# Gates worked out per expert tile from logits in the scattered row, the rank-one term of feature 128 on VectorE, and low parts of the expert weights on GpSimd

## The chip, the cores and the metric

The kernel runs on one core of a Trainium2 chip. The metric is the device time of one execution in microseconds (us). Five engines work side by side, each through its own queue in order: TensorE (PE) multiplies matrices, with its weight loads shown apart as PEld; VectorE (DVE), ScalarE (ACT) and GpSimd (POOL) work on elements; SyncE (SP) issues most of the transfers between the main memory and the on-chip buffer. An engine waits at an instruction until what it needs has been signalled, and what stands behind it in its queue waits too.

## The reference

Three steps follow one another on 8 x 3072 = 24576 tokens of 256 features: the real part of a two-dimensional Fourier transform of each batch, a product layer, and a layer of 8 experts with one expert per token.

```
X = fft(fft(x, axis=1), axis=2).real            # 8 x 3072 x 256
h = ((X @ w1) * (X @ w2)) @ w3 @ w_out          # w1, w2: 256 x 1024, w3: 1024 x 1024, w_out: 1024 x 256
xn = h / (norm(h) + 1e-6);  en = emb / (norm(emb) + 1e-6)
logits = xn @ en.T / tau                        # 8 experts
e = argmax(logits);  gate = softmax(logits)[e]  # sum + 1e-9
out = gate * (relu(h @ ew1[e]) @ ew2[e])        # ew1: 256 x 1024, ew2: 1024 x 256
```

The gate of the chosen expert is 1 / (sum of exp(logit - largest logit) + 1e-9), so it needs the logits and the norm of the token's row.

## The kernel before

Numbers in fp32 are split in a high part, rounded by ScalarE, and a low part, the rest, subtracted by another engine (`split`, lines 112 and 115); a product is then three matmuls (high by high, low by high, high by low). A name that ends in `h` or `l` is such a part.

The program has four stages in the trace. Up to 305 us the Fourier transform runs over the sequence and, beside it, the weights are prepared: `w1` and `w2` are multiplied with the table of the second transform, `w3 @ w_out` is formed, and 8 columns are put behind it that give the logits before the norm. From 305 to 1562 runs the mid stage (`mid`), 24 chunks of 512 columns (tokens), each in 8 iterations. One iteration does three things. `stage_b` makes one slice `f` of 128 of the hidden features: matmuls into `p0`, `q0`, `p1`, `q1` (index 0 for `w1`, 1 for `w2`), sums and differences `a` and `b` of them, and their product `g` for two mirrored sets of columns. `just` splits 128 columns of the previous chunk's `g` into `jh` (ScalarE) and `jl` (POOL), and `stage_c` multiplies them with `wh` and `wl` in 24 matmuls 264 wide into `pc`, which ScalarE copies into `xs`. Two chunks later the router works on `xs`: `choose` finds each token's expert, `place` its slot in the expert's region, and `scatter` writes the token's row there, one indirect DMA of POOL for 128 tokens, 8 for a chunk.

The columns of the Fourier transform are symmetric, so 129 features carry all. Features 0 to 127 go through the matmuls. Feature 128 adds a rank-one term, a row of the columns times a column of the weights. For `w1` VectorE adds it when it empties `p0`: line 781, `ps0 = ub * wcol + p0`, where `ub` is the row in all partitions and `wcol` the weights. For `w2` PE adds it with one more matmul, `p1 <- ur, wrx`, of a three-row operand that is filled by small loads (lines 164 and 165), and ScalarE copies `p1` to `ps1` (line 785). After `stage_c`, ScalarE squares the row of each token with a running sum (line 817). `choose` takes from that the norm (`norm_of`, lines 129 to 139), divides the shifted logits by it (line 850), has ScalarE take the exponential (line 851), sums it and writes the gate behind the row, with the token's number behind that: 258 floats per row.

Beside the first chunks the 64 pieces of the expert weights, 128x512 each, are split by `presplit` (lines 892 to 897): a load `et`, its parts `eh` on ScalarE and `el` on VectorE, and two stores to `dex`. Each of the tiles has two buffers. The order of the engines is made by a scheduler when the program is built, not by the code's order. `mini` does the same work as the loop for one odd column.

After some work between the stages (1562 to 1690, with the first expert's tiles, `lead_tiles`), the expert stage runs over tiles of 256 tokens: `turn` transposes a tile by PE and splits it, `up` multiplies with `ew1` and applies relu while it splits (`hh` on ScalarE, `hl` on VectorE, line 1088), `down` calls `gated` for two halves, which multiplies with `ew2`, scales by the gate from the row (`o`, line 1102) and has POOL write the tokens' rows to the output.

Of the kernel before, what the change touches and what calls it, by code (L numbers as in the profile page):

```python
# [24 lines left out]
XW = 258  # L25
# [34 lines left out]
def fourier_experts(  # L60
# [80 lines left out]
    wcol = const.tile([128, FT], F32, name="wcol")  # L141
# [29 lines left out]
    def open_p1():  # L171
# [12 lines left out]
        wrx = p1c.tile([128, 4 * XW], F32R, name="wrx")  # L184
        nc.gpsimd.memset(wrx.bitcast(F32), 0.0)
        p1["wr"] = wrx[:, 0:F]
        p1["x"] = wrx.rearrange("p (a c) -> p a c", c=XW)
        nc.scalar.dma_start(out=wrx[0:3, 0:F].bitcast(F32), in_=dwr)
# [6 lines left out]
    with ExitStack() as c0:  # L195
        pz = c0.enter_context(tc.tile_pool(name="pz", bufs=2, reuse_waits="tile", space=PSUM))

        def side():
            with tc.tile_pool(name="pw1", bufs=1, reuse_waits="tile") as pe, \
# [7 lines left out]
                yield from prep_in(nc, tc, pr, pz, take, seven, split, prod, three, w1, w2, t_feat, t_row, dwr, wcol, dwc)  # L207
# [7 lines left out]
            nc, tc, c0, pz, split, prod, three, x, x128, xsp, (t_dft, t_pm), p1, du, dv, du128, du128f,  # L215
            dsp, dspx, side(),
        )
    with ExitStack() as c1:
        mid(
            nc, tc, c1, split, prod, three, norm_of, p1, wcol, du128, du128f, dw, dx, dex,  # L220
            ew1, ew2, t_tok, run, eg, lead, ident, out,
        )
# [60 lines left out]
def prep_in(nc, tc, pr, pz, take, seven, split, prod, three, w1, w2, t_feat, t_row, dwr, wcol, dwc):  # L283
    with tc.tile_pool(name="pa1", bufs=1, reuse_waits="tile") as pool, \
# [158 lines left out]
def dft(nc, tc, ctx, pz, split, prod, three, x, x128, xsp, tables, p1, du, dv, du128, du128f, dsp, dspx, side):  # L443
# [190 lines left out]
    def feature128():  # L634
# [24 lines left out]
        for g, c, w in GROUPS:  # L659
# [4 lines left out]
            r8 = [st.tile([NB, 386], F32R if i < 2 else F32, tag="o", name=f"r8{i}") for i in range(3)]  # L664
            split(r8[0][:, 0:n], r8[1][:, 0:n], ps[g][:NB, 0:n])
            nc.scalar.activation(out=r8[2][:, 0:n], in_=ps[g][:NB, 0:n], func=AF.Copy)
            for i, dst in ((2, du128f), (0, du128[:, 0]), (1, du128[:, 1])):
                nc.sync.dma_start(out=dst[:, c:c + w], in_=r8[i][:, 0:w].bitcast(F32))
                if g == 0:
                    nc.sync.dma_start(out=dst[:, H:H + 1], in_=r8[i][:, w:w + 1].bitcast(F32))  # L670
# [43 lines left out]
def mid(  # L714
    nc, tc, ctx, split, prod, three, norm_of, p1, wcol, du128, du128f, dw, dx, dex,
    ew1, ew2, t_tok, run, eg, lead, ident, out,
):
# [49 lines left out]
    def stage_b(f, ops, gt, c):  # L767
        uh, ul, vh, vl, ur, ub = ops
        fs = slice(f * 128, f * 128 + 128)
        ab = []  # L770
# [634 lines left out]
```

## Time and profile before

| | |
|---|---|
| median of 3 runs | 2751.56 us (2749.32 to 2752.73) |
| the profiled execution | 2768.9 us |
| its span, first to last instruction | 2767.2 us |
| mean granted TensorE clock | 0.976 |
| busy in the span: PE, PEld | 2602.1 (94%), 2441.5 (88%) |
| busy in the span: DVE, ACT, POOL | 1690.8 (61%), 1049.5 (38%), 1078.0 (39%) |

PE has work nearly all the time, but an average over four stages does not say which of them has room. Read it by stage: a stage in which PE is busy without a gap moves only with PE's own work; in a stage with gaps, the wait that ends last before PE's next matmul decides. Times in rows are counted from the span's start. "Idle before" with an arrow names what the engine was waiting for.

### The profile page before, as it was taken

What the parts mean: (1) busy time and instruction counts of PE and PEld (TensorE: products, weight loads), DVE (VectorE), ACT (ScalarE), POOL (GpSimd) and SP (SyncE); (2) the same over time, 40 slices, a digit from 0 to 9 for tenths busy, and PEclk for the clock granted to TensorE, in tenths of its full rate; (3) what the DMA queues carried; (4) which work ended last, traced back from release to release, by engine and by line L of the source; (5) the groups of instructions that cost most, each with busy time, mean ns of one, the idle gap of its engine ahead of it and who ended that gap; (6) DMA issues with size and microseconds to landing.
All of it is one profiled execution on the core that took longest, in us unless ns stands there. A gap on an engine that the chain in (4) does not pass through costs nothing.

```text
span 2767.2 us, 48866 instructions
## 1 busy us (share of the span) xinstructions
PE 2602.1 (94%) x18661; PEld 2441.5 (88%) x18661; DVE 1690.8 (61%) x3325; ACT 1049.5 (38%) x2069; POOL 1078.0 (39%) x748
## 2 busy tenths in 40 slices
PE   4988789999999999999999999999999999999998
PEld 3888677877888888888888899999999999999998
DVE  8999389999888878888888852222222222222222
ACT  3554234444434334434344433333333333333332
POOL 5465345565566555565565421111111111111111
PEclk7999899999999999999999999999999999999999
DMA  6766625455211011011010264111111422111110
GB/s 247 242 220 201 199 92 184 164 173 191 73 41 41 28 43 39 28 43 39 28 43 20 108 267 169 47 47 47 47 47 47 163 104 104 47 47 47 47 47 21
DMA packets 114249, 265.07 MB, mean 96 GB/s; under 512 B 16843, under 2 KB 55929, under 8 KB 109148
## 3 DMA queue, kind: packets, MB, share of 16 engines
q1 hardware_dynamic: 84670, 195.58, 21.5%
q0 software_dynamic: 19440, 51.35, 5.2%
q10 hardware_dynamic: 9902, 14.98, 1.5%
q8 instruction: 148, 2.42, 0.4%
q14 instruction: 89, 0.73, 0.1%
HBM read 521.17 MB, written 106.77 MB: 227 GB/s over the span
## 4 chain that ended last, share of the span: by engine, by line
issue 39%; PE 27%; DVE 17%; POOL 11%; DMA 3%; ACT 2%; POOLq 0%; SPq 0%; DVEq 0%; ACTq 0%
PE pc L122 14%; POOL out L1103 7%; PE p L122 6%; PE q L122 5%; DVE b L796 2%; DVE g L799 2%; POOL vl L115 2%; DMA et<-in 2%; DVE a L796 2%; PE acc L122 1%; DVE ps L781 1%; DVE el L115 1%; ACT jh L112 1%; DVE nrm L139 1%; POOL z L504 1%
## 5 line engine op out<-in xcount | busy, mean ns | idle before, releaser
L1088 DVE SCALAR_TENSOR_TENSOR hl<-pd,hh 128x512 fp32r<-128x512 f32 x396 | 273.8, 691 | 783.5 <-ACT hh L1087 752.6
L115 POOL TENSOR_TENSOR jl<-g,jh 128x1024 fp32r<-128x1024 f32 x184 | 443.0, 2409 | 393.9 <-ACT jh L112 330.2
L1103 POOL DMA_INDIRECT out<-o,x x192 | 187.3, 976 | 916.0 <-ACT o L1102 897.2
L122 PE MATMUL pc<-wh,jh 128*128 128x264 f32 x1536 | 449.9, 293 | 53.1 <-ACT xs L815 50.4
L122 PE MATMUL pc<-wh,jl 128*128 128x264 f32 x1536 | 444.1, 289 | 4.1 <-POOL jl L115 4.0
L122 PE MATMUL pc<-wl,jh 128*128 128x264 f32 x1536 | 442.7, 288 | 0.0
L1084 PE MATMUL pd<-xh,wt 128*128 128x256 f32 x2400 | 431.4, 278 | 0.0
L1100 PE MATMUL po<-wt,hh 128*128 128x256 f32 x2400 | 423.9, 280 | 0.0
L112 ACT ACTIVATE jh<-g 128x1024 fp32r<-128x1024 f32 x192 | 203.2, 1059 | 476.4 <-PE pc L122 350.7
L1084 PEld LDWEIGHTS pd<-xh,wt 128*128 128x128 f32 x2400 | 370.0, 188 | 0.0
L122 PEld LDWEIGHTS pc<-wh,jh 128*128 128x128 f32 x1536 | 296.4, 193 | 82.4 <-ACT xs L815 73.3
L1087 ACT ACTIVATE hh<-pd 128x512 fp32r<-128x512 f32 x396 | 236.7, 598 | 339.8 <-PE pd L1084 339.8
L1100 PEld LDWEIGHTS po<-wt,hh 128*128 128x128 f32 x2400 | 364.4, 188 | 0.0
L1100 PE MATMUL po<-wt,hl 128*128 128x256 f32 x1200 | 334.1, 278 | 0.0
L1084 PE MATMUL pd<-xl,wt 128*128 128x256 f32 x1200 | 333.9, 278 | 0.0
L122 PE MATMUL q<-vh,wc 128*128 128x512 f32 x768 | 308.0, 403 | 17.2 <-ACT a L794 10.6
L122 PE MATMUL p<-uh,wc 128*128 128x512 f32 x768 | 308.1, 402 | 3.7 <-DVE ps L781 3.6
L122 PEld LDWEIGHTS pc<-wl,jh 128*128 128x128 f32 x1536 | 296.9, 193 | 5.8
L122 PEld LDWEIGHTS pc<-wh,jl 128*128 128x128 f32 x1536 | 295.9, 193 | 5.6 <-POOL jl L115 5.4
L796 DVE TENSOR_TENSOR b<-ps,q 128x512 f32<-128x512 f32 x384 | 249.0, 688 | 33.9 <-ACT ps L785 20.3
L880 POOL DMA_INDIRECT dx<-xs,idx x192 | 192.5, 1003 | 154.3 <-DVE idx L876 82.0
L799 DVE TENSOR_TENSOR g<-a,b 128x512 f32<-128x512 f32 x384 | 247.6, 679 | 7.7 <-POOL a L796 7.5
(336 smaller groups left out, 5073.4 us busy)
## 6 DMA issues: line engine op xcount, KB each, us to landing
wt<-dex SPq DMA_DIRECT2D x75, 4096.0 KB
wc<-dex SPq DMA_DIRECT2D x22, 4096.0 KB
x<-dx SPq DMA_DIRECT2D x96, 258.0 KB
xt<-in SPq DMA_DIRECT2D x24, 1028.0 KB
et<-in SPq DMA_DIRECT2D x64, 256.0 KB
dex<-eh SPq DMA_DIRECT2D x64, 256.0 KB
dex<-el SPq DMA_DIRECT2D x64, 256.0 KB
raw<-in SPq DMA_DIRECT2D x28, 512.0 KB
```

What stands on the lines that cost most here:

```text
L112: nc.scalar.activation(out=hi, in_=src, func=AF.Copy)
L115: (lo_eng or nc.vector).tensor_tensor(out=lo, in0=src, in1=hi.bitcast(F32), op=ALU.subtract)
L122: nc.tensor.matmul(ps, lhsT=lh, rhs=rh, start=first and i == 0, stop=last and i == n - 1)
L139: nc.vector.scalar_tensor_tensor(out=n_, in0=n_, scalar=0.5, in1=t, op0=ALU.mult, op1=ALU.add)
L796: eng.tensor_tensor(out=t, in0=ps, in1=q, op=o)
L799: nc.vector.tensor_tensor(out=gt[sg][:, f, :], in0=ab[0][sg], in1=ab[1][sg], op=ALU.mult)
L880: i = nc.gpsimd.indirect_dma_start(out=dx, out_offset=bass.IndirectOffsetOnAxis(ap=idx[:, j if k is None else k:][:, 0:1], axis=0), in_=xs ...
L1084: nc.tensor.matmul(ps[:, a, :], lhsT=w[:, lh, o:o + 128], rhs=rh[:, k, :], start=i == 0, stop=i == 5)
L1087: nc.scalar.activation(out=hh[:, sl, :], in_=ps, func=AF.Relu)
L1088: nc.vector.scalar_tensor_tensor(out=hl[:, sl, :], in0=ps, scalar=0.0, in1=hh[:, sl, :].bitcast(F32), op0=ALU.max, op1=ALU.subtract)
L1100: nc.tensor.matmul(ps, lhsT=lh[:, f, sl], rhs=w[:, rh, c:c + D], start=i == 0, stop=i == 3 * FT - 1)
L1103: ins = nc.gpsimd.indirect_dma_start(out=out, out_offset=bass.IndirectOffsetOnAxis(ap=x[:, a, D + 1:D + 2].bitcast(U32), axis=0), in_=o, i ...
```

## The change

Three things change in the code.

- `stage_b` no longer has the matmul of the rank-one term for `w2`, and `ps1` is made as `ps0` was, by VectorE with `ub` and `wcol`, which now holds the column of both weight matrices. The three-row operands, their memory and their small loads go, in `mini` and in the preparation too.
- `choose` no longer works out the gate: the squares, the norm, the exponential and the reciprocals go from the mid stage. The row that `scatter` writes has the 256 features, the 8 logits and the token's number: 265 floats. The new function `gates` works the gates out for one tile of 256 tokens, in `turn` and in `lead_tiles`, and `gated` takes them. The tables of the expert stage share buffers.
- `presplit` has its low part `el` made by POOL.

The diff, cut to its core:

```diff
-XW = 258
+XW = 265
+XP = 272
+TK = 264
...
-    wcol = const.tile([128, FT], F32, name="wcol")
+    wcol = const.tile([128, 2, FT], F32, name="wcol")
...
-        ur = p1["ur"][p]
         ub = pool.tile([128, CH], F32, tag=f"ub{p}", name="ub")
-        nc.sync.dma_start(out=ur[0:1, :].bitcast(F32), in_=du128[b, 0:1, sl])
-        nc.sync.dma_start(out=ur[1:3, :].bitcast(F32), in_=du128[b, :, sl])
         nc.sync.dma_start(out=ub, in_=du128f[b:b + 1, sl].to_broadcast([128, CH]))
-        return ru, rv, ur, ub
+        return ru, rv, ub
...
+                nc.vector.tensor_copy(wcol[:, i, 4 * q:4 * q + 4], ps[:, 0:8:2])
...
-        uh, ul, vh, vl, ur, ub = ops
+        uh, ul, vh, vl, ub = ops
         fs = slice(f * 128, f * 128 + 128)
         ab = []
         for i in range(2):
             pp_ = pp.tile([128, CH], F32, tag=f"p{i}", name=f"p{i}")
-            terms = features(i, 0, f, (uh, ul), "u")
-            if i == 1:
-                terms.append((wr[:, fs], ur))
-            prod(pp_, terms)
+            prod(pp_, features(i, 0, f, (uh, ul), "u"))
             pq = pp.tile([128, CH], F32, tag=f"q{i}", name=f"q{i}")
             prod(pq, features(i, 1, f, (vh, vl), "v"))
             ps = wk.tile([128, CH], F32, tag=f"ps{i}", name=f"ps{i}")
-            if i == 0:
-                nc.vector.scalar_tensor_tensor(
-                    out=ps, in0=ub, scalar=wcol[:, f:f + 1], in1=pp_, op0=ALU.mult, op1=ALU.add
-                )
-            else:
-                nc.scalar.activation(out=ps, in_=pp_, func=AF.Copy)
+            nc.vector.scalar_tensor_tensor(
+                out=ps, in0=ub, scalar=wcol[:, i, f:f + 1], in1=pp_, op0=ALU.mult, op1=ALU.add
+            )
             pair, eng, q = [], nc.vector, pq
...
-        nc.scalar.activation(out=xs[:, j, :], in_=pc, func=AF.Copy)
-        jk = wk.tile([128, D], F32, tag="jk", name="jk")
-        nc.scalar.activation(out=jk, in_=xs[:, j, 0:D], func=AF.Square, accum_out=ss[:, j:j + 1])
+        nc.scalar.activation(out=xs[:, j, 0:TK], in_=pc, func=AF.Copy)
...
-        nrm = small("nrm", 1)[:, :nt]
-        norm_of(nrm, ss[:, :nt], ro, 128, nt, f"n{nt}")
-        nc.vector.tensor_scalar_add(nrm, nrm, 1e-6)
-        inv = small("inv", 1)[:, :nt]
-        nc.vector.reciprocal(out=inv, in_=nrm)
         df = small("df")[:, :nt]
...
-        ex = small("ex")[:, :nt]
-        nc.vector.tensor_tensor(out=df, in0=df, in1=inv.unsqueeze(2).to_broadcast(sh), op=ALU.mult)
-        nc.scalar.activation(out=ex, in_=df, func=AF.Exp)
-        su = small("su", 1)[:, :nt]
-        nc.vector.tensor_reduce(out=su, in_=ex, axis=AX.X, op=ALU.add)
-        nc.vector.tensor_scalar_add(su, su, 1e-9)
-        nc.vector.reciprocal(out=xs[:, 0:nt, D], in_=su)
-        nc.vector.tensor_copy(xs[:, 0:nt, D + 1].bitcast(I32), tok[:, t0:t0 + nt])
+        nc.vector.tensor_copy(xs[:, 0:nt, TK].bitcast(I32), tok[:, t0:t0 + nt])
...
-        split(h, l, t)
+        split(h, l, t, lo_eng=nc.gpsimd)
...
+            gate = gates(nc, ro, wk.tile([128, D], F32, tag="jk", name="jk"), x, norm_of)
...
+def gates(nc, pool, junk, x, norm_of):
+    sh = [128, 2, E]
+    new = lambda nm, *w: pool.tile([128, *w], F32, tag="g" + nm, name="g" + nm)
+    ss, nrm, mx, inv, gate = (new(nm, 2) for nm in ("ss", "nrm", "mx", "inv", "gate"))
+    for a in range(2):
+        nc.scalar.activation(out=junk, in_=x[:, a, 0:D].bitcast(F32), func=AF.Square, accum_out=ss[:, a:a + 1])
+    lg = x[:, :, D:D + E].bitcast(F32)
+    nc.vector.tensor_reduce(out=mx, in_=lg, axis=AX.X, op=ALU.max)
+    norm_of(nrm, ss, pool, 128, 2, "gn")
+    nc.vector.tensor_scalar_add(nrm, nrm, 1e-6)
+    nc.vector.reciprocal(out=inv, in_=nrm)
+    df = new("df", 2, E)
+    nc.vector.tensor_tensor(out=df, in0=lg, in1=mx.unsqueeze(2).to_broadcast(sh), op=ALU.subtract)
+    nc.vector.tensor_tensor(out=df, in0=df, in1=inv.unsqueeze(2).to_broadcast(sh), op=ALU.mult)
+    ex = new("ex", 2, E)
+    nc.scalar.activation(out=ex, in_=df, func=AF.Exp)
+    nc.vector.tensor_reduce(out=gate, in_=ex, axis=AX.X, op=ALU.add)
+    nc.vector.tensor_scalar_add(gate, gate, 1e-9)
+    nc.vector.reciprocal(out=gate, in_=gate)
+    return gate
...
-    nc.scalar.activation(out=o, in_=ps, func=AF.Copy, scale=x[:, a, D:D + 1].bitcast(F32))
+    nc.scalar.activation(out=o, in_=ps, func=AF.Copy, scale=gate[:, a:a + 1])
...
+    gtp = pool("xg", 3)
...
+        gts[p] = gates(nc, gtp, ip.tile([128, D], F32, tag="jk", name="jk"), xts[p], norm_of)
```

What the scheduler makes of it stands in three places.

The order of POOL in the mid stage while expert weights are split; before, there is no `el` on it (`jl` is the low part for `stage_c`, `dx` the rows of the scatter):

```order
L115 TENSOR_TENSOR jl_4856<-g0_4182,jh_4855 128x1024
L115 TENSOR_TENSOR jl_4919<-g0_4182,jh_4918 128x1024
L115 TENSOR_TENSOR jl_5028<-g0_4182,jh_5027 128x1024
L115 TENSOR_TENSOR jl_5110<-g0_4182,jh_5109 128x1024
L880 DMA dx_67<-xs_4184,idx_5076 198912x258 x6
L115 TENSOR_TENSOR jl_5187<-g1_4183,jh_5186 128x1024
L880 DMA dx_67<-xs_4184,idx_5076 198912x258 x2
L115 TENSOR_TENSOR jl_5256<-g1_4183,jh_5255 128x1024
```

And after, the same place:

```order
L114 TENSOR_TENSOR el_9190<-et_9187,eh_9189 128x512
L114 TENSOR_TENSOR el_9335<-et_9332,eh_9334 128x512
L114 TENSOR_TENSOR jl_4925<-g0_4087,jh_4924 128x1024
L114 TENSOR_TENSOR el_9485<-et_9482,eh_9484 128x512
L114 TENSOR_TENSOR el_9638<-et_9635,eh_9637 128x512
L829 DMA dx_65<-xs_4089,idx_4892 198912x265 x5
L114 TENSOR_TENSOR jl_4999<-g1_4088,jh_4998 128x1024
L829 DMA dx_65<-xs_4089,idx_4892 198912x265 x3
L114 TENSOR_TENSOR el_9775<-et_9772,eh_9774 128x512
L114 TENSOR_TENSOR el_9920<-et_9917,eh_9919 128x512
L114 TENSOR_TENSOR jl_5065<-g1_4088,jh_5064 128x1024
```

Two `el` now stand ahead of nearly each `jl`, and the eight scatters of a chunk are parted 5 and 3 around a `jl`. After 31 `jl` the last `el` is done.

The order of VectorE in one plain iteration of the mid stage (`p` and `q` are what PE filled), before:

```order
L781 SCALAR_TENSOR_TENSOR ps_10482<-ub,wcol,p_10474 128x512
L796 TENSOR_TENSOR a_10484<-ps_10482,q_10478 128x512
L796 TENSOR_TENSOR a_10485<-ps_10482,q_10478 128x512
L796 TENSOR_TENSOR b_10499<-ps_10497,q_10493 128x512
L796 TENSOR_TENSOR b_10500<-ps_10497,q_10493 128x512
L799 TENSOR_TENSOR g_9918<-a_10484,b_10499 128x512
L799 TENSOR_TENSOR g_9919<-a_10485,b_10500 128x512
```

And after:

```order
L746 SCALAR_TENSOR_TENSOR ps_11030<-ub,wcol,p_11022 128x512
L759 TENSOR_TENSOR a_11032<-ps_11030,q_11026 128x512
L759 TENSOR_TENSOR a_11033<-ps_11030,q_11026 128x512
L746 SCALAR_TENSOR_TENSOR ps_11044<-ub,wcol,p_11036 128x512
L759 TENSOR_TENSOR b_11046<-ps_11044,q_11040 128x512
L759 TENSOR_TENSOR b_11047<-ps_11044,q_11040 128x512
L762 TENSOR_TENSOR g_10515<-a_11032,b_11046 128x512
L762 TENSOR_TENSOR g_10516<-a_11033,b_11047 128x512
```

The second `ps` stands between the `a` and the `b`; ScalarE, which made it before, has only `jh` and `xs` by turns in such iterations.

The order of VectorE in the expert stage after, from one `hl` to the next tile's first step (names with `g` ahead are those of `gates`; before, only `hl` and `xl` stood here):

```order
L1030 SCALAR_TENSOR_TENSOR hl<-pd,hh 128x512
L128 TENSOR_SCALAR gnh<-gss 128x2
L131 TENSOR_SCALAR gnrm<-gnh 128x2
L136 RECIPROCAL gnq<-gnrm 128x2
L137 SCALAR_TENSOR_TENSOR gnq<-gnq,gss 128x2
L1030 SCALAR_TENSOR_TENSOR hl<-pd,hh 128x512
L138 SCALAR_TENSOR_TENSOR gnrm<-gnrm,gnq 128x2
L136 RECIPROCAL gnq<-gnrm 128x2
L137 SCALAR_TENSOR_TENSOR gnq<-gnq,gss 128x2
L138 SCALAR_TENSOR_TENSOR gnrm<-gnrm,gnq 128x2
L136 RECIPROCAL gnq<-gnrm 128x2
L1030 SCALAR_TENSOR_TENSOR hl<-pd,hh 128x512
```

Three to five small steps now stand between two `hl`.

## Rows read from the trace of the kernel before

**Rows 1.** Stages: length, busy (x instructions) by engine, PEclk, DMA share, GB/s

```profile
364.00:569.00 205.00, 187.95 (x1116) 164.04 (x1117) 189.70 (x365) 89.34 (x188) 103.19 (x60) 0.95 0.47 157
569.00:692.00 123.00, 115.30 (x703) 99.23 (x702) 114.74 (x213) 58.65 (x122) 69.17 (x41) 1.00 0.55 179
692.00:1511.00 819.00, 781.81 (x4871) 696.26 (x4872) 678.61 (x1384) 330.76 (x690) 471.45 (x286) 0.99 0.12 39
...
1690.00:2757.00 1067.00, 1066.57 (x9228) 1066.37 (x9226) 308.30 (x458) 352.12 (x644) 180.51 (x185) 1.00 0.19 61
```

**Rows 2.** Line 781 by stretch, one instruction per iteration

```profile
364.00:569.00 205.00, 22.05 (x30) 0.95 0.47 157
569.00:692.00 123.00, 13.65 (x19) 1.00 0.55 179
692.00:1511.00 819.00, 94.30 (x128) 0.99 0.12 39
```

**Rows 3.** Timeline of PE: start, us, engine, line, operation, count

```profile
1096.11 0.40 PE L122 MATMUL p<-uh,wc 128*128 128x512 f32 x1
...
1098.20 0.40 PE L122 MATMUL p<-ur,wrx 128*128 128x512 f32 x1
1098.44 0.39 PE L122 MATMUL q<-vh,wc 128*128 128x512 f32 x1
...
1102.07 0.40 PE L122 MATMUL p<-uh,wc 128*128 128x512 f32 x1
```

**Rows 4.** Waits of PE, 692 to 1511: total, times, longest

```profile
PE pc L122 <- ACT xs L815: 34.3, 28, 2.5
```

**Rows 5.** Waits of DVE, 692 to 1511

```profile
DVE ps L781 <- PE q L122: 47.1, 16, 3.6
```

**Rows 6.** Timeline of ACT, mid stage

```profile
1123.57 0.26 ACT L851 ACTIVATE ex<-df 128x64 f32<-128x64 f32 x1 [2.59 <-DVE df L850]
```

**Rows 7.** Groups of DVE, 692 to 1511: busy, mean ns, idle before, releasers

```profile
L781 DVE SCALAR_TENSOR_TENSOR ps<-ub,wcol,p 128x512 f32<-128x512 f32 x128 | 94.6, 739 | 107.2 <-PE p L122 59.1 <-PE q L122 47.1 <-PE pc L122 0.9
L138 DVE SCALAR_TENSOR_TENSOR n8q<-n8q,ss 128x8 f32<-128x8 f32 x48 | 23.2, 484 | 0.0
...
L132 DVE TENSOR_SCALAR nrm<-n8h 128x8 int32<-128x8 int32 x16 | 2.6, 160 | 0.0
```

**Rows 8.** Timeline of DVE, mid stage

```profile
1115.34 0.20 DVE L137 RECIPROCAL n8q<-nrm 128x8 f32<-128x8 f32 x1
1115.46 0.70 DVE L781 SCALAR_TENSOR_TENSOR ps<-ub,wcol,p 128x512 f32<-128x512 f32 x1
1116.07 1.53 DVE L138 SCALAR_TENSOR_TENSOR n8q<-n8q,ss 128x8 f32<-128x8 f32 x1
```

**Rows 9.** Timeline of POOL, mid stage

```profile
1115.15 2.42 POOL L115 TENSOR_TENSOR jl<-g,jh 128x1024 fp32r<-128x1024 f32 x1 [3.49 <-ACT jh L112]
...
1132.88 0.98 POOL L880 DMA_INDIRECT dx<-xs,idx  x1 [0.30 <-issue]
```

**Rows 10.** Groups of POOL, 692 to 1511

```profile
L115 POOL TENSOR_TENSOR jl<-g,jh 128x1024 fp32r<-128x1024 f32 x128 | 308.3, 2409 | 258.4 <-ACT jh L112 202.3 <-PE p L122 55.4
...
L115 POOL TENSOR_TENSOR ul<-ru,uh 128x512 fp32r<-128x512 f32 x15 | 19.5, 1298 | 0.0
```

**Rows 11.** Timeline while expert weights are split (SPq issues DMAs)

```profile
474.31 1.18 SPq L892 DMA_DIRECT2D et<-in  x2
...
478.75 1.27 ACT L112 ACTIVATE eh<-et 128x512 fp32r<-128x512 f32 x2 [2.70 <-DMA et<-in]
...
479.41 1.33 DVE L115 TENSOR_TENSOR el<-et,eh 128x512 fp32r<-128x512 f32 x2 [0.81 <-ACT eh L112]
...
481.47 1.03 SPq L892 DMA_DIRECT2D et<-in  x2
```

**Rows 12.** Groups, expert stage, 1690 to 2757

```profile
L1088 DVE SCALAR_TENSOR_TENSOR hl<-pd,hh 128x512 fp32r<-128x512 f32 x368 | 254.6, 692 | 754.4 <-ACT hh L1087 723.5 <-issue 30.8
```

**Rows 13.** Timeline of DVE, between mid and expert stage

```profile
1600.37 0.16 DVE L138 SCALAR_TENSOR_TENSOR n2q<-n2q,ss 128x2 f32<-128x2 f32 x1
```

More of the change, by code (lines that the diff above doesn't have):

```diff
@@ L183, in open_p1 @@
             nc.sync.dma_start(out=p1["l"][:, q, :].bitcast(F32), in_=dwc[1, :, q, :])
[L184 to L188, printed above, removed]
+        wrx = p1c.tile([128, 4 * XP], F32R, name="wrx")
+        p1["x"] = wrx.rearrange("p (a c) -> p a c", c=XP)
         p1["uh"] = p1c.tile([128, NB], F32R, name="umh")
@@ L206, in side @@
                 )
-                yield from prep_in(nc, tc, pr, pz, take, seven, split, prod, three, w1, w2, t_feat, t_row, dwr, wcol, dwc)
+                yield from prep_in(nc, tc, pr, pz, take, seven, split, prod, three, w1, w2, t_feat, wcol, dwc)
                 enT = embed(nc, pe, pz, norm_of, ident, emb, tau)
@@ L219, in fourier_experts @@
         mid(
[L220 removed]
+            nc, tc, c1, split, prod, three, norm_of, p1, wcol, du128f, dw, dx, dex,
             ew1, ew2, t_tok, run, eg, lead, ident, out,
@@ L225, in fourier_experts @@
         c2.enter_context(tc.manual_schedule(engines={mybir.EngineType.SP}))
-        experts(nc, tc, c2, p1["w"], p1["xs"], ident, run, t_g, eg, lead, dx, dex, out)
+        experts(nc, tc, c2, norm_of, p1["w"], p1["xs"], ident, run, t_g, eg, lead, dx, dex, out)
     left2.close()
@@ L280, in narrow_split, with prep_in @@
     nc.vector.tensor_tensor(out=lo, in0=c, in1=hi.bitcast(F32), op=ALU.subtract)
-def prep_in(nc, tc, pr, pz, take, seven, split, prod, three, w1, w2, t_feat, t_row, dwr, wcol, dwc):
+def prep_in(nc, tc, pr, pz, take, seven, split, prod, three, w1, w2, t_feat, wcol, dwc):
     with tc.tile_pool(name="pa1", bufs=1, reuse_waits="tile") as pool, \
@@ L663, in feature128 @@
             n = w + 1 if g == 0 else w
[L664 to L670, printed above, removed]
+            r8 = st.tile([NB, 386], F32, tag="o", name="r8")
+            nc.scalar.activation(out=r8[:, 0:n], in_=ps[g][:NB, 0:n], func=AF.Copy)
+            nc.sync.dma_start(out=du128f[:, c:c + w], in_=r8[:, 0:w])
+            if g == 0:
+                nc.sync.dma_start(out=du128f[:, H:H + 1], in_=r8[:, w:w + 1])
             yield
@@ L932, in mini_out @@
     def mini_out(hl):
-        xs = xsp.tile([128, 8, 264], F32, tag="xs", name="xsm")
-        ss = ro.tile([128, 8], F32, tag="ss", name="ssm")
-        stage_c(hl, xs, ss, 0)
-        idx = place(*choose(xs, ss, 1, NCH * 8, True))
+        xs = xsp.tile([128, 8, XW], F32, tag="xs", name="xsm")
+        stage_c(hl, xs, 0)
+        idx = place(*choose(xs, 1, NCH * 8, True))
         scatter(xs, idx, 0)
@@ L1002, in mid @@
                 p1["xs"] = [p1["x"][:, 0:2, :], p1["x"][:, 2:4, :]] + [
-                    p1["raw"].tile([128, 2, XW], F32R, tag=t, name="xl") for t in ("ru", "rv")
+                    p1["raw"].tile([128, 2, XP], F32R, tag=t, name="xl") for t in ("ru", "rv")
                 ]
@@ L1023, in mid @@
                     stage_c(*late)
-                late = (hl, xs, ss, i) if gprev is not None else None
+                late = (hl, xs, i) if gprev is not None else None
                 if c == 1 and i == 1:
@@ L1108, in gated, with experts @@
     tc.add_to_no_dep_group("outs", ins)
-def experts(nc, tc, ctx, w0, x0, ident, run, t_g, eg, lead, dx, dex, out):
+def experts(nc, tc, ctx, norm_of, w0, x0, ident, run, t_g, eg, lead, dx, dex, out):
     pool = lambda nm, n, **k: ctx.enter_context(tc.tile_pool(name=nm, bufs=n, reuse_waits="tile", **k))
@@ L1232, in table @@
         sh = [1, n, E]
-        cm = cp.tile(sh, F32, name=f"cm{a}")
+        cm = cp.tile(sh, F32, tag="cm", name=f"cm{a}")
         nc.vector.tensor_tensor(
@@ L1249, in table @@
         nc.vector.tensor_copy(tab[:, 0, :], te)
-        ch = cp.tile([1, n], F32, name=f"ch{a}")
+        ch = cp.tile([1, n], F32, tag="ch", name=f"ch{a}")
         nc.vector.memset(ch[:, 0:1], 1.0)
```

114 lines of the change are left out of this document (40 added, 74 removed).

## The prediction

> **What bounds the kernel now.** I read the stage table first, then inside the mid stage the waits and the timelines of single engines, and last the expert stage. From 1690 to 2757 us PE is busy 1066.57 of 1067 us [rows 1]: nothing but PE work counts there, and the change takes none away. The change acts in the mid stage, between 364 and 1562. There PE is busy 781.81 of 819 us after 692, and 187.95 of 205 us in the stretch where the expert weights are still being split [rows 1]. Line 781 runs once per iteration, so its counts tell how many iterations a stretch holds: 30, 19 and 128 [rows 2], that is 6.83, 6.47 and 6.40 us each, or 51.2 us per chunk of 8 after 692. An iteration in which PE never waits takes 1102.07 − 1096.11 = 5.96 us [rows 3], 47.7 us per chunk; with the small `place` matmuls, which I put at 0.3, it is 48.0. The remaining 3.2 us per chunk are waits. The table of PE waits names `xs` on ScalarE for 34.3 us in 28 waits [rows 4], 2.1 per chunk. So the steady mid stage is PE plus some waits on ScalarE, whose own work is small; VectorE is second, at 678.61 / 16 = 42.4 us per chunk [rows 1].
>
> **The change, part by part.** All sums are made against the profiled run, 2768.9 us (span 2767.2), which is 0.6% above the median of 2751.56; the result is scaled by that ratio at the end.
>
> *The rank-one matmul goes.* It starts at 1098.20 and the next one at 1098.44 [rows 3]: 0.24 us per iteration, on the path wherever PE is the bound. The unstalled iteration becomes 5.72, the chunk 45.8 + 0.3 = 46.1.
>
> *VectorE takes over `ps1`.* One scalar_tensor_tensor of the kind of line 781, 739 ns [rows 7], less the overlap with its neighbour: 0.70 [rows 8], 5.6 us per chunk. ScalarE loses a copy and, since the norm goes, a Square and an accumulator read per iteration; ScalarE is not the bound, so this is worth only what PE waited for it.
>
> *The router gives up the norm and the exponential.* Eleven groups leave VectorE in the mid stage, from 23.2 us (`n8q`, 48 instructions) down to 2.6 us [rows 7], 98.0 us together, 6.1 per chunk. Small instructions overlap: the reciprocal at 1115.34 takes 0.20 and its successor starts 0.12 later [rows 8]. So the gain lies between 0.6 × 6.1 = 3.7 and 6.1; I take 3.7. VectorE per chunk is then 42.4 + 5.6 − 3.7 = 44.3, under PE's 46.1 but near it.
>
> *Waits of PE.* The Exp on ScalarE waited 2.59 us for VectorE with the next `xs` behind it [rows 6], and PE waited for that `xs`. This head-of-line wait goes with the Exp. The other recurring wait stays possible: once per chunk VectorE waits about 47.1 / 16 = 2.9 us for a signal of PE [rows 5], at the burst of scatters that POOL issues 1.28 us apart [rows 9]; I can't explain it. If one of PE's 28 waits lies there in each chunk, at their mean of 34.3 / 28 = 1.2 us [rows 4], it costs 1.2 per chunk. Of the 3.2 us of waits I thus let the chunk keep between 0.3 (the Exp and the burst both gone, since the new order breaks the burst into 5 and 3) and 3.7 (VectorE the bound, rival B). I take 1.8, between the chunk in which VectorE's 44.3 and its 2.9 add up, 47.2, and PE's 46.1 with the burst's 1.2 and the 1.1 kept for which I have no name (3.2 − 2.1), 48.4. The chunk is 47.9.
>
> *Expert weights' low parts move to POOL.* This is the term against the change. Before, a pair of 128x512 loads is issued at 474.31, ScalarE rounds it at 478.75, VectorE subtracts at 479.41, and the next pair is issued at 481.47 [rows 11]: a cycle of 7.2 us, of which 4.44 is the load. The loads stand in SP's queue behind the stores of the pair before, and those behind the subtract, so this is a chain. On POOL the same shape takes 1298 ns [rows 10] instead of 0.67: from eh to the next load is 478.75 to 481.47 = 2.72 now; with 0.63 us more for each of the two subtracts it is about 4.0, and with a load of 4.2 the cycle is 8.2. The order of the changed kernel puts one pair before nearly each `jl`, seven pairs per chunk; `jl` (2409 ns [rows 10]) comes behind the pair on POOL, and PE's `pc` matmuls wait for `jl`. So PE runs at the pair's pace while it lasts, 26.5 pairs, 217 us. To that I add 10 for the 3.5 iterations without a pair, which can make up part of their time, and 22 for three places where scatters stand among the pairs (4 × 1.28 = 5.1, twice, with `jl` and a pair 15.4 instead of 8.2 each). The 30 iterations of 364 to 569 then take 249 to 260 us; I take 250: a loss of 45. Bounds: with the cycle of before, 7.2, the loss is 18; with the cycle hidden under PE it is a small gain; with everything on POOL one behind the other it is near 100 (rivals). POOL has the time as such, busy only 103 of 205 us [rows 1]; it is the order that costs. After it the iterations of 569 to 692 no longer carry any split.
>
> *Gates in the expert stage.* Per tile about 19 small VectorE instructions of 0.16 to 0.2 us [rows 13], 3 to 4 us, two Squares and one Exp on ScalarE, beside PE's 11.6 us per tile (four `hl` per tile, so 92 tiles [rows 12] in 1067 us). VectorE is busy 308.30 of 1067 us, ScalarE 352.12 [rows 1], and `hl` is idle before it for 754.4 us [rows 12]. PE hides it: cost 0. If the cover fails, each 0.2 us per tile costs 18 us. Wider rows (265 floats for 258) and the lost small loads I cost at nothing: DMA share is 0.12 and 0.19 there [rows 1]. In the change of stages, gates stand ahead of the expert table on VectorE; I allow 1 us.
>
> **Sum.** 364 to 569: +45. 569 to 692: 19 iterations at 47.9 / 8 = 5.99 are 114 instead of 123, −9. 692 to 1511: 16 × (51.2 − 47.9) = −53. The last chunk −3. Between the stages +1. Net −19: 2749.9 against 2768.9, a ratio of 0.9931, and 2751.56 × 0.9931 = 2733 us.
>
> **Rivals.** *A, slower: POOL's queue is one chain.* If `jl` does not fit into the load's 4.2 us because its `jh` comes late behind both roundings on ScalarE, each el waits for it and the cycle is 4.2 + 1.3 + 2.6 + 2.4 = 10.5. Then 26.5 × 2.3 = 61 more: 2811, scaled 2793. It decides from a cycle of 8.2 + 19 / 26.5 = 8.9 on. Against it: 2.4 fits into 4.2 if `jh` is on time. *B, slower: VectorE is the bound after 692.* `n8q` at 1116.07 took 1.53 us and ended with POOL's `jl`, 1117.6, while `ps`, with one operand in PSUM, took 0.70 [rows 8, 9]. If about 2.6 us of such waits come back per chunk on top of 44.3 + 2.9, the chunk is 49.8: 1.9 × 19.4 chunks = 37 more, 2787, scaled 2769. It decides from 48.9. The Trainium skill, "SBUF — State Buffer", section "Who interferes with whom", states that a VectorE instruction with two inputs in SBUF and a GpSimd instruction that reads SBUF exclude each other for the whole of the one that started first; the two rows agree, and by that rule all two-input steps of the router that remain would be held by el and jl alike, which is rival B. *C, faster: the split is hidden.* If only POOL's own work counts, 2 × 1.3 for el, 2.4 for `jl`, 1.28 for one scatter and 0.3 for a share of `ul` and `vl`, 6.6 per iteration, the 30 iterations take 198 us and the 45 shrink to 0 at least: 2705, scaled 2688. *D, no change: the gates cost PE 0.2 us per tile*, through VectorE's queue ahead of `hl`: 18 more, 2768, scaled 2751. Against it: PE has no wait in the whole expert stage.
>
> **How the numbers follow.** Forecast (2715 to 2745) 0.47, C 0.17, A 0.14, B 0.10, D 0.12. Faster by over 0.2% (about what a measurement of this kernel can tell from no change): 0.64; within: 0.12; slower: 0.24. The range leaves out half of A and the fastest of C: 2690 to 2775; the likeliest case's own is 2715 to 2745.
>
> **What would show it.** Right: the stretch of 30 iterations with the split near 250 us, PE waiting there for `jl` behind el; after it 47 to 48.5 us per chunk, with no wait behind an Exp; the expert stage unchanged to 1 us per 100. Wrong: a pair cycle near 7 or above 9, VectorE busy throughout a late chunk, or any PE wait among the experts.

## The result and the profile after

The changed kernel takes 2791.16 us (median, 2782.78 to 2795.5) against 2750.44 of the kernel before: a ratio of 1.0143, interval 1.0118 to 1.0169, so it is 1.4% slower, where 2733 had been predicted. The profiled execution took 2795.5 us (span 2793.7), 4 us above its median; that of before took 2768.9 (span 2767.2), 18 us above the median of its own runs. So the two traces differ by 26.5 us where the medians differ by 41. What made the trace of before the longer one of its kind can't be seen in it. Page of the changed kernel, part 1:

```profile
span 2793.7 us, 49657 instructions
...
PE 2573.5 (92%) x18485; PEld 2425.1 (87%) x18485; DVE 1967.5 (70%) x4894; ACT 934.3 (33%) x1958; POOL 1141.4 (41%) x808
```

PE has 28.6 us less to do than before, and VectorE 277 us more. The stages of the changed kernel (stretch, length, busy time by engine, granted clock of PE, DMA share, GB/s), to be held against [rows 1]:

```profile
364.00:569.00 205.00, 173.60 (x1010) 150.70 (x1010) 166.16 (x268) 67.98 (x109) 153.84 (x102) 0.92 0.63 208
569.00:692.00 123.00, 113.97 (x689) 100.91 (x688) 106.99 (x183) 32.26 (x50) 79.40 (x52) 0.94 0.24 83
692.00:1511.00 819.00, 747.17 (x4699) 667.18 (x4699) 734.20 (x1227) 190.64 (x286) 468.00 (x283) 0.96 0.11 36
1700.00:2680.00 980.00, 980.00 (x8451) 980.00 (x8451) 493.61 (x2035) 398.86 (x1018) 165.63 (x171) 1.00 0.21 68
```

The expert stage is as full as it was. In the stretch from 692 to 1511 PE is busy 747 instead of 782 us; its granted clock is 0.96 instead of 0.99. Line 746, which is line 781 of before, now stands twice in an iteration:

```profile
364.00:692.00 328.00, 68.13 (x93) 0.93 0.48 161
692.00:1511.00 819.00, 185.97 (x253) 0.96 0.11 36
```

From 692 on that is 126.5 iterations where [rows 2] count 128: 6.47 us each, 51.8 per chunk. The chunk of 47.9 us has not come about, though the matmul is gone. The starts of line 746 give the chunks one by one: between 715 and 1542 us, 7 of them take 48.1 to 49.2 us and 9 take 53.2 to 54.9. What PE waits for there (total, times, longest), and what VectorE waits for:

```profile
PE q L121 <- DVE a L759: 61.9, 9, 7.5
PE pc L121 <- POOL jl L114: 7.2, 11, 1.1
```

```profile
DVE xs L805 <- issue: 54.2, 10, 6.7
DVE xs L805 <- DMA dx<-xs,idx: 14.1, 6, 6.5
DVE ps L746 <- PE p L121: 5.9, 23, 0.4
```

Nothing of this kind stood in [rows 4, 5]. Nine times PE waits some 6.9 us for `a`, which VectorE would make, and VectorE itself waits at line 805. This is `xs<-tok`, the step that writes the token's number behind the row. In front of the casts VectorE's queue holds 88 wait instructions of this line, and the longest of them lasted 8.3 us:

```profile
L805 DVEq EVENT_SEMAPHORE  x88: 21/50/8277, 467.8 to 1583.3; - x88
```

This fits the table above, which names no releaser ("issue") for ten of the 16 waits: there a wait instruction ahead of the cast took the last signal. One such place, VectorE and then POOL:

```profile
1203.52 0.74 DVE L746 SCALAR_TENSOR_TENSOR ps<-ub,wcol,p 128x512 f32<-128x512 f32 x1
1210.80 2.73 DVE L805 CAST xs<-tok 128x8 int32<-128x8 f32 x1 [6.53 <-DMA dx<-xs,idx]
```

```profile
1206.51 0.99 POOL L829 DMA_INDIRECT dx<-xs,idx  x1 [0.31 <-issue]
1207.81 0.98 POOL L829 DMA_INDIRECT dx<-xs,idx  x1 [0.30 <-issue]
1208.81 4.69 POOL L114 TENSOR_TENSOR jl<-g,jh 128x1024 fp32r<-128x1024 f32 x2
```

VectorE ends a `ps` at 1204.26. In its queue the cast comes next; it starts at 1210.80, after the landing of the last scatter, which POOL issued at 1207.81, and then takes 2.73 us. Only behind it, at 1213.44, does VectorE make the second `ps`, and at 1214.10 the `a` that PE waits for: 9.2 us go by between the two `ps`. The order of the changed kernel shows why the cast waits for a scatter (three rows out of VectorE's list, in this order):

```
L825 CAST idx_10735<-sl_10732 128x8
L805 CAST xs_11101<-tok_3116 128x8
L789 TENSOR_REDUCE mx_11222<-xs_10517 128x8
```

The token of buffer `xs_11101` is written ahead of the router's first step on `xs_10517`, the chunk before it. There are two such buffers, so `xs_11101` is the memory that the scatters behind `idx_10735` are just reading. Before, the token went to column 257 of a row of 264, which ScalarE's copy of `pc` fills whole; the cast had to come after the copy, and stood inside `choose`. Now it goes to column 264, and the copy fills only 0 to 263. Nothing ties the cast to the copies any more, and here the scheduler put it as early as the buffer can be had.

The wait costs more than its length. Granted clock (third number from the end) after it:

```profile
1175.00:1204.00 29.00, 29.00 (x192) 26.19 (x191) 28.67 (x54) 7.53 (x11) 16.00 (x10) 1.00 0.07 27
...
1211.00:1217.00 6.00, 1.57 (x4) 1.29 (x5) 6.00 (x7) 0.00 (x0) 2.50 (x2) 0.55 0.00 0
1217.00:1222.00 5.00, 5.00 (x32) 4.59 (x31) 4.79 (x9) 0.00 (x0) 0.00 (x0) 0.86 0.00 0
1222.00:1228.00 6.00, 6.00 (x39) 5.43 (x38) 5.79 (x10) 2.85 (x5) 4.83 (x3) 1.00 0.04 8
```

```profile
1208.36 0.40 PE L121 MATMUL p<-uh,wc 128*128 128x512 f32 x1
1215.43 0.80 PE L121 MATMUL q<-vh,wc 128*128 128x512 f32 x1 [6.67 <-DVE a L759]
1216.45 0.63 PE L121 MATMUL q<-vh,wc 128*128 128x512 f32 x1
...
1218.74 0.40 PE L121 MATMUL q<-vh,wc 128*128 128x512 f32 x1
```

PE has no work from 1208.76 to 1215.43. Read microsecond by microsecond, its granted clock is 1.00 up to 1211, 0.50 from 1212 to 1218, which is the lower of its two levels (1.2 and 2.4 GHz), and 1.00 again from 1219. So the clock falls in the wait and comes back some 3 us after PE has work again. The eight matmuls from 1215.43 on take 3.3 us; eight of the same kind take 1.8 at full clock (1222.13 to 1223.97). A wait of 6.7 us thus costs some 1.5 us more. The Trainium skill, "TensorE: Matmul & The Clock Gate", "Part 1: The HAM clock gate", describes a clock that is cut when PE has been idle; these rows agree, 0.50 in and behind a wait of 6.67 us.

### The profile page after: what moved, and what is told of

Same layout as the page of the kernel before. It is cut to its first block, busy times and chain, and to the rows that moved or that the text cites. A ratio compares the mean times of both kernels' runs of the same rounds, so it can differ in the third digit from the quotient of the medians.

```text
span 2793.7 us, 49657 instructions
## 1 busy us (share of the span) xinstructions
PE 2573.5 (92%) x18485; PEld 2425.1 (87%) x18485; DVE 1967.5 (70%) x4894; ACT 934.3 (33%) x1958; POOL 1141.4 (41%) x808
## 4 chain that ended last, share of the span: by engine, by line
issue 44%; PE 26%; POOL 14%; DVE 9%; DMA 5%; ACT 1%; POOLq 1%; SPq 0%; ACTq 0%; DVEq 0%
PE pc L121 12%; POOL out L1067 7%; PE q L121 6%; PE p L121 5%; DMA et<-in 3%; POOL dx L829 2%; POOL vl L114 2%; POOL el L114 2%; PE acc L121 2%; DVE xs L805 1%; DMA du<-o 1%; DVE a L759 1%; DVE ps L746 1%; DMA dx<-xs,idx 1%; POOL jl L114 1%
## 5 line engine op out<-in xcount | busy, mean ns | idle before, releaser
L121 PE MATMUL pc<-wh,jh 128*128 128x264 f32 x1536 | 444.1, 289 | 23.9 <-ACT xs L778 21.5
L1064 PE MATMUL po<-wt,hh 128*128 128x256 f32 x2400 | 434.0, 283 | 0.0
L121 PE MATMUL q<-vh,wc 128*128 128x512 f32 x768 | 319.4, 417 | 99.0 <-DVE a L759 77.3
L746 DVE SCALAR_TENSOR_TENSOR ps<-ub,wcol,p 128x512 f32<-128x512 f32 x384 | 281.8, 742 | 27.9 <-PE p L121 27.0
L121 PEld LDWEIGHTS q<-vh,wc 128*128 128x128 f32 x768 | 151.8, 198 | 151.3 <-DVE a L759 86.3
```

The lines of the kernel that those rows point to most:

```text
L121: nc.tensor.matmul(ps, lhsT=lh, rhs=rh, start=first and i == 0, stop=last and i == n - 1)
L746: nc.vector.scalar_tensor_tensor(out=ps, in0=ub, scalar=wcol[:, i, f:f + 1], in1=pp_, op0=ALU.mult, op1=ALU.add)
L1064: nc.tensor.matmul(ps, lhsT=lh[:, f, sl], rhs=w[:, rh, c:c + D], start=i == 0, stop=i == 3 * FT - 1)
```

## Experiments

The runs were made in four sets (e1 to e4; e5 and e7 to e9; e6, e10 and e11; e12), each with the kernel before beside it, whose median went from 2753 to 2758 us (2750 beside the changed kernel). Ratios are to it; a difference between runs of different sets is safer taken from the ratios.

**e1, the token step tied.** Only this is changed in the changed kernel:

```diff
-        nc.vector.tensor_copy(xs[:, 0:nt, TK].bitcast(I32), tok[:, t0:t0 + nt])
+        nc.vector.scalar_tensor_tensor(
+            out=xs[:, 0:nt, TK].bitcast(I32), in0=mx, scalar=0.0, in1=tok[:, t0:t0 + nt], op0=ALU.mult, op1=ALU.add
+        )
```

> The changed kernel, with the token number written as 0 x (largest logit) + token instead of a plain cast, so that this step can't stand ahead of the chunk's own logits. Theory T (the early cast, which waits for the scatters of the same buffer, holds VectorE's queue): the 9.9 and 13.9 us iterations vanish, every chunk after 692 takes 48 to 49.5 us instead of 48.1 to 54.9, and the time is about 2791 - 9 x 5.1 - 28 = 2717 us (2705 to 2735). Rival A (POOL's el is what costs): the stretch from 425 to 612 us keeps its 61 to 64 us per chunk, and the time is no lower than 2745. Rival B (VectorE is the bound whatever the cast does): late chunks stay above 51 us and the time is 2780 to 2795.

Measured: 2697.30 us, ratio to the kernel before 0.980 (0.9783 to 0.9817): 94 us less than the changed kernel, more than any theory said. Waits of PE and VectorE from 649 to 1439 us, 17 chunks; then line 746 by stretch (32 and 136 iterations):

```profile
PE pc L121 <- POOL jl L114: 9.1, 17, 0.6
```

```profile
DVE ps L746 <- PE p L121: 29.9, 55, 1.1
```

```profile
364.00:602.00 238.00, 46.79 (x64) 0.93 0.60 203
649.00:1439.00 790.00, 199.63 (x272) 1.00 0.12 41
```

A chunk takes 790 / 17 = 46.5 us, all of them alike, and PE waits 0.5 us in each. The theory of the early cast holds, and rival B (VectorE as the bound) falls. Rival A's sign, chunks of 61 to 64 us where the split is crowded, was there in part: three chunks between 422 and 606 us take 64.6, 59.5 and 60.5. The time fell all the same, far under A's 2745. In the stretch with el, 364 to 602, an iteration takes 238 / 32 = 7.44 us, against 6.83 before and 8.33 in the prediction (250 / 30).

**e2 and e3, el back on VectorE,** with the step tied (e2) and with the early cast (e3):

```diff
-        split(h, l, t, lo_eng=nc.gpsimd)
+        split(h, l, t)
```

> As the kernel with the tied token step, and the low part el back on VectorE as before. It prices el on POOL without the early cast. Theory T with el on POOL costing little: within 10 us of the kernel with the tied step, about 2717. Rival A: 25 to 45 us faster than that one, because the chain through POOL goes.

> The changed kernel with el back on VectorE and the early cast left as it is. Theory T: the late chunks keep their 53 to 55 us, so the time stays within 15 us of the changed kernel, 2775 to 2795. Rival A: 2745 to 2765, since the loss between 364 and 612 goes.

Measured: e2 2713.10 us, ratio 0.9847 (0.9828 to 0.9865), 16 us slower than e1; e3 2734.47 us, ratio 0.992 (0.9896 to 0.9945). In either run both expectations missed. Moving el back gains nothing, so rival A is out by e2. What el on POOL gains can't be read from e2, though: with el on VectorE the scheduler also put the eight scatters of 13 chunks in one burst, where e1 has them 4 and 4 around a `jl`. e6 below has POOL's order fixed and is the cleaner price.

In e3 nothing ties the cast, and yet it mostly did not move. It stands right behind the first router step of its own chunk, as at 735 us, and runs ahead of that step only in the last chunks, as at 1361:

```profile
735.26 0.21 DVE L789 TENSOR_REDUCE mx<-xs 128x8 f32<-128x64 f32 x1
735.40 2.27 DVE L805 CAST xs<-tok 128x8 int32<-128x8 f32 x1
...
1361.05 2.93 DVE L805 CAST xs<-tok 128x8 int32<-128x8 f32 x1 [1.52 <-issue]
1379.36 0.21 DVE L789 TENSOR_REDUCE mx<-xs 128x8 f32<-128x64 f32 x1
```

The four chunks from 1281 us on take 47.8, 48.2, 54.2 and 54.8 us, where e2's take 46.3 to 46.6. That is 19 of the 21 us between e3 and e2. So e3 doesn't show that the early cast is cheap beside el on VectorE; it shows that only the chunks in which the cast runs ahead pay for it.

**e4, no rank-one term for w2 at all:** e1 with `ps1` copied by ScalarE, as before, and no matmul.

```diff
-            nc.vector.scalar_tensor_tensor(
-                out=ps, in0=ub, scalar=wcol[:, i, f:f + 1], in1=pp_, op0=ALU.mult, op1=ALU.add
-            )
+            if i == 0:
+                nc.vector.scalar_tensor_tensor(
+                    out=ps, in0=ub, scalar=wcol[:, i, f:f + 1], in1=pp_, op0=ALU.mult, op1=ALU.add
+                )
+            else:
+                nc.scalar.activation(out=ps, in_=pp_, func=AF.Copy)
```

> As the kernel with the tied token step, but ps1 is copied by ScalarE and the rank-one term of w2 is left out altogether. It takes 0.74 us per iteration off VectorE and adds a copy to ScalarE. If PE is the bound of a late chunk: within 0.5 us per chunk of the kernel with the tied step. If VectorE is: up to 2 us per chunk less (46.5 instead of 48.5), 30 to 45 us in all.

Measured: 2768.01 us, ratio 1.0052 (1.0035 to 1.0070), 71 us slower than e1 with less work in it, which neither answer allowed. Waits of PE:

```profile
PE pc L121 <- POOL jl L114: 40.1, 15, 3.5
```

With another length of the steps the scheduler put all eight scatters of a chunk in one burst, 1069 to 1079 us in one chunk, with `jl` behind it; in e1 they stand 4 and 4 around a `jl`. So e4 doesn't price VectorE's work. It shows what stands beside a burst of eight: late chunks of 49.4 us on average (15 in 740.4 us) instead of 46.5, some 2.7 us of waiting for `jl` in each, and a clock of 0.98 over these chunks instead of 1.00. The burst was not tried by itself with everything else as in e1.

**e7, the burst in the kernel before,** with POOL in the order of the code in the mid stage, which spreads the scatters 2, 2, 1, 2, 1:

```diff
     with ExitStack() as c1:
+        c1.enter_context(tc.manual_schedule(engines={mybir.EngineType.Pool}))
         mid(
```

> The kernel before, only with POOL's queue in the mid stage in the order of the code, so that the scatters stand 2, 2, 1, 2, 1 over five iterations instead of 6 + 2 or 7 + 1 around one jl. If the burst of scatters is what makes VectorE and PE wait once per chunk, the late chunks fall from 51.2 to 48 to 49.5 us and the time to 2705 to 2725. If the waits for xs come from the exponential's place on ScalarE alone, the chunk stays above 50.5 and the time above 2740.

Measured: 2757.45 us, ratio 1.0009 (1.0000 to 1.0019). Late chunks fell, 10 of 15 to 48.7 to 49.1 us, but the chunks with el, between 361 and 699 us, took 338 instead of 328. VectorE's wait for PE at the burst, [rows 5], is gone from the late stretch; PE still waits for `xs`:

```profile
PE pc L122 <- ACT xs L816: 20.1, 16, 2.5
```

So the burst was part of the late chunk's waits, as supposed, but spreading it alone is worth nothing in the total, and why the chunks with el got longer stays open.

**e8 and e9, one part alone.** Each is the kernel before with one part of the diff: the rank-one term (e8: no matmul, `ps1` by VectorE), or the gates and the longer row (e9, early cast included). **e11** is e9 with the token step of e1.

> The kernel before with the rank-one part of the change alone: no matmul for it, ps1 by VectorE; the router and el as before. PE's unstalled iteration is 5.72, but the order now has all eight scatters in one burst and VectorE keeps the norm. Bounds: PE's gain alone is 24 x 1.9 = 46 us, 2708; if the burst of 8 costs as in the run with the copy on ScalarE (48.2 to 51.0 us per late chunk), 2725 to 2750; if VectorE with 42.4 + 5.6 = 48.0 and the burst's wait is the bound (52 us), 2765.

> The kernel before with the gates part of the change alone; the rank-one matmul stays on PE and el on VectorE. The token's cast moves ahead of its chunk here too, and the scatters stand in one burst of 8. If the early cast and the burst cost as in the changed kernel, late chunks take 52 to 56 us and the time is 2770 to 2800; if it needs VectorE's second ps to hurt, chunks stay near 50 and the time is 2730 to 2755. The expert stage is to stay at 1067 us in both.

> The gates part alone, with the tied token step; the order of POOL is the same as in the run of the gates part alone (2866 us). Theory T: the 14.4 us iteration of each chunk falls to 6 to 9, chunks come to 48 to 51 us, and the time to 2740 to 2765; the burst of 8 scatters is still there. If the burst and not the early cast made the 14.4, it stays above 2840.

Measured: e8 2746.08 us, ratio 0.9966 (0.9951 to 0.9980). e9 2866.39 us, ratio 1.0409 (1.0392 to 1.0426). e11 2751.16 us, ratio 0.9968 (0.9955 to 0.9980). In e8, with the norm still on VectorE and el there too, that engine is the bound (692 to 1097 us: DVE, the third busy time, 403 of 405):

```profile
692.00:1097.00 405.00, 381.80 (x2323) 323.81 (x2322) 403.23 (x774) 146.05 (x307) 232.22 (x142) 1.00 0.30 96
```

In e9 each late chunk has one iteration of 14.4 us; PE's waits:

```profile
PE q L124 <- DVE b L798: 91.9, 15, 7.2
```

Neither expectation for e9 reached that far. POOL's order is the same in e9 and e11, with the burst of eight in most chunks of both, so the 4.4% between them, some 120 us, are the early cast's. Alone, each part is worth 0.3% (e8, e11); together (e2) 1.5%, all three with bursts of eight in most chunks. The expert stage is filled by PE in all of them.

**e10, early but short:** the changed kernel with the token written by a reduction over one element, as early as the cast.

```diff
-        nc.vector.tensor_copy(xs[:, 0:nt, TK].bitcast(I32), tok[:, t0:t0 + nt])
+        nc.vector.tensor_reduce(
+            out=xs[:, 0:nt, TK].bitcast(I32), in_=tok[:, t0:t0 + nt].unsqueeze(2), axis=AX.X, op=ALU.max
+        )
```

> The changed kernel with the token number written by a reduction over one element in place of the cast; it stands as early as the cast does, but it has one operand in the on-chip buffer and took 0.2 us elsewhere, where the early cast took 2.7 to 3.1 us beside POOL's jl. It parts the early step's wait for the scatters (1.4 to 6.5 us) from its own length. If the wait is what costs: most of the long iterations stay, at about 7 instead of 9.9 us, and the time is 2735 to 2775. If the length is: the time comes to 2697 to 2715, that of the tied step. If neither part can be taken away alone: about 2791.

Measured: 2747.57 us, ratio 0.9958 (0.9943 to 0.9973). Line 805 of the changed kernel, then of e10 (duration in ns, least, median, most):

```profile
L805 DVE CAST xs<-tok x26: 147/2857/3108, 331.2 to 1590.4; 128x8 int32<-128x8 f32 x23, 128x2 int32<-128x2 f32 x2, 128x4 int32<-128x4 f32 x1
```

```profile
L805 DVE TENSOR_REDUCE xs<-tok x26: 133/168/169, 323.3 to 1531.6; 128x8 int32<-128x8 f32 x23, 128x2 int32<-128x2 f32 x2, 128x4 int32<-128x4 f32 x1
```

The step shrinks from 2.86 to 0.17 us, good chunks to 46.5, and about half of the 94 us go: 44 by the times, 51 by the ratios. The wait for the scatters stays, and with it the other half: bad chunks still take 52 to 53. The cast was long because POOL worked beside it, as `n8q` in [rows 8, 9]. At 1210.80 it ended at 1213.53 and the two `jl` at 1213.50, and so it is at every early cast: the long ones end within 0.05 us of a `jl` or el. The same cast in the kernel before:

```profile
L856 DVE CAST xs<-tok x26: 162/176/2380, 432.5 to 1599.6; 128x8 int32<-128x8 f32 x23, 128x2 int32<-128x2 f32 x2, 128x4 int32<-128x4 f32 x1
```

It took 0.16 to 0.18 us in 24 places without POOL work beside it, and 2.2 to 2.4 in the two where a `jl` ran. A cast has one operand in the buffer; the Trainium skill, "SBUF — State Buffer", "Who interferes with whom", names cast among the operations that can take the port pair shared with GpSimd, and says that reductions do not: the two rows agree.

**e5, e6 and e12, the pace of the expert weights.** e5 is e1 with POOL in the order of the code, by the line of e7: one el for two iterations, scatters spread. e6 is e5 with el on VectorE. e12 is e5 with ScalarE in the order of the code too, and the loads issued from its queue an iteration ahead:

```diff
+    def preload(n):
+        if n >= 8 * E:
+            return
+        e, w, q = n // 8, n // 4 % 2, n % 4
+        ets[n] = exp_.tile([128, 512], F32, tag="et", name="et")
+        nc.scalar.dma_start(out=ets[n], in_=(ew2 if w else ew1)[e, :, q * 512:(q + 1) * 512])
...
-                if i % 2 == 1:
+                if i % 2 == 0:
+                    preload(n)
+                else:
                     presplit(n)
```

> The kernel with the tied token step (2697 us), with POOL's queue in the mid stage in the order of the code: one el for every two iterations, the scatters 2, 2, 1, 2, 1 over five iterations. There, three chunks with seven pairs each took 59.5 to 64.6 us against 46.5 without. If it is the crowding of el ahead of jl that costs, nearly all chunks come to 46.5 to 48 us and the time falls by 30 to 45 us, to 2652 to 2667. If the loads' chain through SP costs whatever the pace, 16 chunks have 4 el each and take over 49, and the time is 2690 or more.

> The fastest kernel so far (tied token step, POOL in the order of the code, 2663 us) with the low part el on VectorE instead. If el on POOL is worth something by itself, as the pair 2713 against 2697 says, it is 10 to 25 us slower, 2673 to 2688. If that pair only showed the different pace of the two orders, it is within 5 us.

> The fastest kernel so far (2663 us: tied token step, POOL in the order of the code), with the loads of the expert weights issued from ScalarE's queue one iteration ahead of their rounding, and ScalarE in the order of the code. There PE waited 29.5 us for xs that stood behind a rounding that waited for its load, and a chunk with four el took 48.0 to 48.5 us against 45.7 without. If the late load is the cause, those chunks come to 46 to 46.7 and the time to 2630 to 2645; if el itself or the contention of its transfers is, they stay at 48 and the time within 5 us of 2663.

Measured: e5 2662.91 us, ratio 0.9669 (0.9653 to 0.9685); e6 2688.74 us, ratio 0.9740 (0.9722 to 0.9759), some 20 us slower than e5 by the ratios; e12 2621.28 us, ratio 0.9515 (0.9495 to 0.9535). The stretch with el and a late one, in e5 and in e12:

```profile
465.00:1046.00 581.00, 555.62 (x3567) 498.01 (x3566) 528.53 (x928) 168.01 (x266) 417.57 (x265) 1.00 0.31 105
1092.80:1366.90 274.10, 274.10 (x1783) 249.94 (x1782) 263.62 (x465) 71.84 (x109) 181.04 (x110) 1.00 0.14 44
```

```profile
470.00:1060.00 590.00, 590.00 (x3837) 537.96 (x3837) 573.11 (x999) 184.47 (x286) 449.96 (x285) 1.00 0.33 111
1100.00:1370.00 270.00, 270.00 (x1754) 246.17 (x1754) 261.58 (x458) 70.04 (x107) 174.85 (x107) 1.00 0.13 39
```

Late chunks are full of PE in both, 274.1 / 6 = 45.7 us each. With el they take 581 / 12 = 48.4 in e5 and as much as without in e12, where PE has no gap. So what a split cost was neither POOL's work nor the traffic. The crowding ahead of `jl`, which e5 was made to try, was not it either. PE's wait in e1's three crowded chunks, ScalarE's from 417 to 602 us, the stretch itself, and e5's wait of PE from 305 to 1700 us:

```profile
PE pc L121 <- ACT xs L778: 32.7, 12, 8.4
```

```profile
ACT eh L111 <- DMA et<-in: 97.8, 25, 12.1
```

```profile
421.90:606.50 184.60, 151.96 (x910) 135.26 (x909) 135.87 (x233) 58.74 (x94) 141.16 (x95) 0.92 0.60 204
```

```profile
PE pc L121 <- ACT xs L779: 29.5, 29, 2.1
```

In those chunks PE has no wait for `jl` in the table. It waits for `xs`, which stands on ScalarE behind a rounding `eh` that waits for its load `et`. e5 has nearly as much of this wait, but in pieces of at most 2.1 us where e1 has up to 8.4. Its clock is 1.00 and not 0.92, and PE is busy 46.3 us per chunk (555.62 / 12) and not 50.7 (151.96 / 3). Late chunks also lose their wait for `jl`, 46.5 to 45.7 us, with the scatters spread. The 34 us from e1 to e5 are made of these; e5 changed the pace of el and the scatters together, and how much is due to each is not shown. e12 takes most of the wait for `xs` away (29.5 to 1.0 us) and 42 us with it, more than was expected; it changed the queue of the loads, their time and ScalarE's order at once, and these too were not tried one by one. VectorE is 261.6 of 270 us busy there; little is left. e12 beats both kernels; 4.85% against the kernel before.

## Why the prediction was wrong

- *What the step left out.* This is the step that failed. "The router gives up the norm and the exponential" counted what leaves VectorE and took the rest of `choose` to stay where it stood. The cast of the token did not. It moved a whole chunk ahead and took on a wait for eight scatters, in VectorE's queue, ahead of all that PE needs. No term was there for it. It was worth 94 us as a whole (e1), against a forecast of −19 and a result of +41. The order of VectorE showed the move, and the working listed the instructions of `choose` without looking up where each stood.
- *The chunk of 47.9 us.* Without the cast it is 46.5 (e1) and, with POOL in the order of the code, 45.7 (e5): the unstalled iteration of 5.72 was right, at 5.71. The mid value between bounds was too high, since both named waits went, as the lower bound of 0.3 us had it.
- *VectorE's 44.3 us per chunk.* In e1 it is busy 747 of 790 us, that is 44.0 per chunk. The term was right, and VectorE is near the bound but not it.
- *el on POOL, +45.* Both the size and the wait were wrong. The prediction had PE wait for `jl` behind el on POOL. From 305 to 692 us of the changed kernel PE waits for `xs` on ScalarE, and hardly for `jl`:

```profile
PE pc L121 <- ACT xs L778: 21.0, 13, 8.4
...
PE pc L121 <- POOL jl L114: 3.4, 4, 1.3
```

  In e1 an iteration in that stretch takes 7.44 us instead of 8.33; against before this is +18 for 30 iterations, and the next 16 iterations, free of el, give 16 back. Against el on VectorE, with POOL in the order of the code, it is a gain of some 20 us (e6). The chain of loads through SP was there, but it reached PE through the rounding on ScalarE, and VectorE's el had cost as much.
- *Rival A* named 2793 us and the result is 2791. That is chance: where el stands, PE waited for `jl` only 3.4 us, and with el moved back but the step tied (e2, e6) the time gets longer.
- *The gates beside the experts: 0.* Right: from 1700 to 2680 PE is busy 980 of 980 us, with VectorE at 494 and ScalarE at 399.

Between the traces the account closes without the cast as well: e1 is 78 us shorter than before, 76 of it in the 16 chunks that before took from 692 to 1511.

## What to carry to other kernels

When a change narrows what one instruction writes, look for every other writer of that buffer: a tie that kept it in place may have gone with the columns. Then find each instruction that stays in the new order, not only those that come and go, and ask of any that moved ahead what it will wait for and who stands behind it in its queue. Work that is off the critical path should be paced by hand where the scheduler bunches it; here this was worth more (e1 to e12, 76 us) than the change with its step tied (e1, 2% of the time).

## What the runs showed of the hardware

In a wait of PE of 6.7 us its granted clock fell to 0.50, and it stayed there for some 3 us of the work behind the wait, so that eight matmuls took 3.3 us instead of 1.8. A cast of 128x8 took 0.16 to 0.18 us with no work on POOL beside it (before) and up to 3.1 us, 2.86 in the median, beside POOL's subtracts (changed kernel), ending within 0.05 us of one of them; where two `jl` stood back to back it ended with the second. A reduction of the same shape in the same place in the order took 0.17. Eight scatters issued one after another stood 1.29 us apart and held POOL's queue for 10 us (e4, 1069 to 1079), and PE waited some 2.7 us per chunk for the `jl` behind them.
